# w2 transposed by DMA transposes on SyncE instead of on TensorE, and the products for M one step later

## Chip, cores and metric

The kernel runs on one core of a Trainium2 chip. The metric is the device time of one execution in microseconds (us). Before the change it is 490.49 us, the median of 3 runs (489.95 to 490.56).

## What is computed

```python
def _attn_ref(x, filt_r, filt_i):              # x: 8 x 3072 x 256
    X = np.fft.rfft(x, axis=1)
    F = (filt_r + 1j * filt_i)[None, :, :]
    return np.fft.irfft(X * F, n=x.shape[1], axis=1)

def _moe_ref(x, w1, w2, w_out):                # x: 24576 x 256, w1, w2: 256 x 1024, w_out: 1024 x 256
    h1 = x @ w1
    h2 = x @ w2
    g = np.maximum(h1, h2)
    return g @ w_out
```

The first function mixes along the sequence, with a filter in the frequency domain. Its result, reshaped to 24576 x 256, goes through the second.

## The kernel before

**The second part is rewritten.** Because max(h1, h2) = max(h1 - h2, 0) + h2, the kernel keeps the difference Wd = w1 - w2 and the product M = w2 @ w_out (256 x 256), and computes relu(y @ Wd) @ Wo + y @ M. So w2 itself is needed only for Wd and for M. To compute M on TensorE, w2 must lie with its 1024 columns on the partitions: that is w2T, w2 transposed.

**The work is a list of steps written out by hand.** After a setup (tables, and the mixing of batch 0), a loop runs over 64 tiles `tt` of 384 rows (8 per batch) and 8 steps `j` in each; step 8 * i + j of batch b is named (b, step). At each step the loop emits `moe_h(tt, j)` (two matmuls at L656, their ReLU on ScalarE at L661 or VectorE at L658), then what the dictionary `mid` holds for the step, then some matmuls of `moe_o(tt - 1, ...)` (L720 with Wo, L718 with M), then what `todo` holds for it, in the order in which `plan(b, step, fn, ...)` was called. Every engine takes its own instructions in this order, with no scheduler in between; semaphores only make it wait.

**Around the change**, in batch 0:

- GpSimd casts the second weight to bf16 in two halves, `cast_w2` (L327), into `w2b`. These casts come after its loads of x for batch 1 (L125), the load of w_out (L330) and the four pieces of Wd (L334).
- `prep_t(jp)` (L336) handles one of these halves: eight 128 x 128 transposes on TensorE into a PSUM tile (L341), and one eviction on ScalarE into `w2T` (L342). `prep_t(0)` is planned at step 7; `prep_t(1)` stands in `mid[0, 8]`, ahead of step 8's L720.
- `prep_m` (L344), at step 9, multiplies w2T by w_out: 16 matmuls (L348) and an eviction into M on ScalarE (L350). M is first read by L718 in step 12.
- `f1(1, c)` (L366, evicted at L369 or L371, stored on SyncE at L374 after every second c) is the first stage of batch 1, at steps 5 to 12. `f1_read` (L380) reads the stored rows back at step 13, and L435 uses them as `bt` from step 25 on. L366 of c = 8 to 11 reads the x tile of one GpSimd load, and of c = 12 to 15 that of the next.
- `load_xf` (L130, L134) on SyncE loads x of batch 2 from step 8 on; GpSimd's `fold` (L140, L141) takes these tiles, and L397 multiplies them from step 25 on.
- `t2` (L793) are other transposes on TensorE, for batch 0.

All SyncE DMAs go out in program order; a DMA whose input isn't ready holds up those behind it. At step 9, `prep_m` is planned ahead of `f1`, so its matmuls stand ahead of that step's L366.

Of the kernel before, what the change touches and what calls it, by code (L numbers as in the profile page):

```python
# [9 lines left out]
BF16 = mybir.dt.bfloat16  # L10
AF = mybir.ActivationFunctionType
# [4 lines left out]
D = 256  # L16
# [11 lines left out]
def kernel(  # L28
# [14 lines left out]
    nc = tc.nc  # L43
    V, S, G, TE = nc.vector, nc.scalar, nc.gpsimd, nc.tensor
# [11 lines left out]
    I128 = const.tile([128, 128], BF16)  # L56
# [3 lines left out]
    w2b = pfpool.tile([128, 2, HID], BF16, tag="pf", name="w2b")  # L60
    w2T = pfpool.tile([128, 8, D], BF16, tag="pf", name="w2T")
# [11 lines left out]
    ps = banks.enter_context(tc.tile_pool(name="ps", bufs=6, space=bass.MemoryType.PSUM))  # L73
# [35 lines left out]
    def plan(b, step, fn, *a):  # L109
        todo.setdefault((b + step // 64, step % 64), []).append((fn, a))  # L110
# [223 lines left out]
        engine.tensor_tensor(Wd[:, :, js], w1f[:, :, js], w2f[:, :, js], OP.subtract)  # L334

    def prep_t(jp):  # L336
        pt = ps.tile([128, 4, D], BF16, tag="ps", name="pt")
        for ji in range(4):
            for dc in range(2):
                j = 4 * jp + ji  # L340
                TE.transpose(pt[:, ji, 128 * dc:128 * dc + 128], w2b[:, dc, 128 * j:128 * j + 128], I128)  # L341
        S.activation(w2T[:, 4 * jp:4 * jp + 4], pt, AF.Copy)  # L342

    def prep_m():  # L344
        pm_ = ps.tile([128, 2, D], FP32, tag="ps", name="pm_")
# [566 lines left out]
    mid = {}  # L912
# [12 lines left out]
                plan(b, n, s1_read, b + 2, v)  # L925

    plan(0, 1, t2, 1, (V,))
    plan(0, 7, prep_t, 0)
    plan(0, 9, prep_m)
    for c, n in ((2, 7), (4, 22), (5, 32), (6, 40), (7, 48)):  # L930
        plan(0, n, t2, c, (V,))
    plan_f1(0, 1, (5, 6, 7, 7, 9, 9, 10, 10, 11, 11, 12, 12), 13)
# [37 lines left out]
    for b in range(B + 1):  # L970
        for i in range(8):
# [12 lines left out]
            assert sum(n) == 30  # L984
            share[b, i] = n

    mid[0, 8] = [(t2, (3, (V,))), (prep_t, (1,))]

    for tt in range(8 * B + 1):
        if tt == 7:  # L990
# [58 lines left out]
```

## Time and profile before

| | |
|---|---|
| median of 3 runs | 490.49 us |
| the profiled execution's own time | 489.1 us |
| its span, first to last instruction | 487.3 us |
| mean granted TensorE clock | 0.993 |
| w2b casts on GpSimd, L327 | 2 x 1.04 us, from 40.16 us |
| transposes of w2, L341 | 16, from 41.25 to 43.8 us |
| ScalarE evictions into w2T, L342 | 2 x 1.02 us |
| products for M, L348 | 16, from 45.0 to 46.6 us |

The profile shows one execution. PE is TensorE's matmuls, PEld its weight loads, DVE VectorE, ACT ScalarE, POOL GpSimd; SPq are the DMAs that SyncE issues. A row of the timeline gives start, length, engine, line, operation, and in brackets the idle time before it with what released it. The chain of work that ended last is followed back from the end of the run; its pieces add up without overlap, while matmul rows of the timeline overlap because matmuls are pipelined. A row of the stages gives the stretch, its length, busy time of the five engines with instruction counts, the granted TensorE clock (1.00 is full speed), the mean busy share of the 16 DMA engines, and GB/s.

### The profile page before, as it was taken

How to read it: one execution, taken by the hardware profiler on the slowest of the kernel's cores; microseconds unless marked ns; L12 is line 12 of the kernel's file. 1: busy time of each engine (PE TensorE's matmuls, PEld its weight loads, DVE VectorE, ACT ScalarE, POOL GpSimd, SP SyncE). 2: the span in 40 equal slices, each digit the busy share in tenths (PEclk: the TensorE clock that was granted, in tenths of full speed). 3: DMA queues.
4: the chain of work that ended last, by engine and by line, in shares of the span. 5: the costliest groups of instructions: out<-in, count | busy, mean ns of one | idle time of the engine just before them, and what ended most of it. 6: DMA issues, size and time to landing. Idle time of an engine off the chain costs nothing.

```text
span 487.3 us, 15411 instructions
## 1 busy us (share of the span) xinstructions
PE 475.9 (98%) x6204; PEld 342.3 (70%) x6207; DVE 362.4 (74%) x589; ACT 307.4 (63%) x645; POOL 296.0 (61%) x378
## 2 busy tenths in 40 slices
PE   8689999999999999999999999999999999999996
PEld 4457777776677676776677676776777776777775
DVE  7886789987876878677786778777885878775542
ACT  5877488667764778468764677467774556354442
POOL 8695868559980698739874698738951266111110
PEclk9979999999999999999999999999999999999999
DMA  8999999898766889789876897789556523541112
GB/s 124 172 247 228 263 255 270 272 254 241 216 180 193 214 270 282 222 237 265 234 187 199 237 261 222 221 245 248 169 165 213 175 88 107 174 156 66 66 66 86
DMA packets 87816, 97.37 MB, mean 200 GB/s; under 512 B 9281, under 2 KB 67938, under 8 KB 87650
## 3 DMA queue, kind: packets, MB, share of 16 engines
q1 hardware_dynamic: 79010, 79.30, 57.7%
q0 software_dynamic: 8592, 17.01, 13.8%
q8 instruction: 48, 0.79, 0.7%
q14 instruction: 22, 0.18, 0.1%
q10 hardware_dynamic: 144, 0.09, 0.1%
HBM read 53.87 MB, written 47.19 MB: 207 GB/s over the span
## 4 chain that ended last, share of the span: by engine, by line
PE 93%; DVE 2%; DMA 2%; POOL 1%; issue 1%; ACT 0%; DVEq 0%; POOLq 0%
PE po L720 36%; PE ph L656 34%; PE po L718 9%; PE pc L612 3%; PE pa L403 2%; PE pz L547 2%; PE px L493 2%; DMA xb<-in_x_dram 2%; DVE pq L441 1%; DVE F L164 1%; PE pr L793 1%; POOL xb L125 1%; PE pz L459 1%; PE pa L366 1%; PE py L629 1%
## 5 line engine op out<-in xcount | busy, mean ns | idle before, releaser
L720 PE MATMUL po<-Wo,gt 128*128 128x256 bf16 x1528 | 263.1, 273 | 0.0
L661 ACT ACTIVATE gt<-ph 128x384 bf16<-128x384 f32 x347 | 165.9, 502 | 141.6 <-PE ph L656 136.8
L720 PEld LDWEIGHTS <-gt 128*128 128x128 bf16 x1528 | 144.2, 98 | 66.4 <-issue 12.4
L658 DVE TENSOR_SCALAR gt<-ph 128x384 bf16<-128x384 f32 x165 | 90.6, 552 | 46.2 <-PE ph L656 44.5
L656 PEld LDWEIGHTS <-Wd 128*128 128x128 bf16 x1024 | 99.0, 98 | 14.1 <-DVE pf L507 0.7
L668 POOL DMA_DIRECT2D out_dram<-ot x86 | 48.8, 568 | 98.1 <-DVE ot L731 87.8
L140 POOL TENSOR_TENSOR xb<-XF 128x512 bf16<-128x512 f32 x48 | 61.1, 1274 | 51.3 <-DMA XF<-in_x_dram 44.4
L503 DVE TENSOR_TENSOR pf<-px,F 128x1024 f32<-128x1024 f32 x60 | 71.1, 1218 | 18.7 <-PE px L493 7.0
L731 DVE TENSOR_SCALAR ot<-po 128x512 f32<-128x512 f32 x83 | 57.0, 686 | 18.8 <-PE po L720 18.2
L141 POOL TENSOR_TENSOR xb<-XF 128x512 bf16<-128x512 f32 x48 | 61.0, 1272 | 0.0
L407 ACT ACTIVATE at<-pa 128x512 bf16<-128x512 f32 x96 | 50.0, 603 | 4.0 <-PE pa L403 3.1
L533 POOL TENSOR_TENSOR ri<-pf 128x256 bf16<-128x256 f32 x60 | 43.8, 730 | 14.3 <-DVE pf L503 14.1
L534 POOL TENSOR_TENSOR ri<-pf 128x256 bf16<-128x256 f32 x60 | 43.6, 727 | 0.0
L556 ACT ACTIVATE zt<-pz 128x512 bf16<-128x512 f32 x60 | 31.3, 600 | 9.2 <-PE pz L547 9.2
L617 ACT ACTIVATE ce<-pc 128x384 f32<-128x384 f32 x56 | 23.7, 490 | 3.5 <-PE pc L612 2.1
L441 DVE TENSOR_TENSOR pq<-px,F 128x1024 bf16<-128x1024 f32 x19 | 22.1, 1219 | 2.6 <-PE px L435 2.3
L403 PE MATMUL pa<-xb,CT 64*32 64x512 bf16 x320 | 16.2, 381 | 0.0
L612 PEld LDWEIGHTS <-zr 48*128 48x128 bf16 x896 | 12.6, 93 | 4.4 <-issue 3.6
L612 PE MATMUL pc<-G,zr 48*128 48x48 bf16 x896 | 14.8, 180 | 0.0
L493 PE MATMUL px<-bt,U 64*32 64x256 bf16 x432 | 14.4, 272 | 0.0
L514 DVE TENSOR_TENSOR pf<-px,F 128x1024 f32<-128x1024 f32 x6 | 7.4, 1226 | 5.0 <-POOL ri L534 4.3
L804 PE MATMUL pd<-W 128*128 128x512 bf16 x26 | 9.5, 496 | 1.5 <-DVE zero L186 1.5
(415 smaller groups left out, 735.5 us busy)
## 6 DMA issues: line engine op xcount, KB each, us to landing
XF<-in_x_dram SPq DMA_DIRECT2D x96, 192.0 KB
out_dram<-ot SPq DMA_DIRECT2D x101, 128.0 KB
out_dram<-ot POOLq DMA_DIRECT2D x90, 128.0 KB, 3.5
ad<-at SPq DMA_DIRECT2D x56, 192.0 KB
zd<-zt SPq DMA_DIRECT2D x42, 256.0 KB
bt<-ad SPq DMA_DIRECT2D x72, 128.0 KB
zr<-zd SPq DMA_DIRECT2D x24, 192.0 KB
zr<-zd SPq DMA_DIRECT2D x28, 96.0 KB
```

The lines of the kernel that those rows point to most:

```text
L140: G.tensor_tensor(t_[:, 0], f[:, 0], f[:, 1], OP.add)
L141: G.tensor_tensor(t_[:, 1], f[:, 0], f[:, 1], OP.subtract)
L407: S.activation(at[:, m0:m0 + 2], pa[g], AF.Copy)
L503: V.tensor_tensor(t_, px[s].rearrange("p (o k) d -> p o k d", o=1).to_broadcast([128, 2, 2, D]), F[:, :, 2 * n, s].rearrange("p c (o d) -> ...
L533: G.tensor_tensor(ri[:, s, 0], t_[:, 0, 0], t_[:, 1, 1], OP.subtract)
L656: TE.matmul(ph, Wd[:, dc, 128 * j:128 * j + 128], y_[:, dc], start=(dc == 0), stop=(dc == 1))
L658: V.tensor_scalar(gt[tt][:, j], ph, 0.0, None, OP.max)
L661: S.activation(gt[tt][:, j], ph, AF.Relu)
L668: E.dma_start(out=dst, in_=src)
L718: TE.matmul(p_, y_[:, n, blk], M[:, n], start=(e == 0), stop=(e == 9))
L720: TE.matmul(p_, g_[:, n - 2, blk], Wo[:, n - 2], start=(e == 0), stop=(e == 9))
L731: V.tensor_scalar(ot[tt // 2][:, e - 1:e + 1], po[q // 2 % 2], SCALE, None, OP.mult)
```

## The change

`prep_t` no longer uses TensorE, PSUM or ScalarE: for each half of w2 it issues two DMA transposes on SyncE, from w2b straight into w2T. The halves are planned at steps 3 and 4 instead of 7 and 8, so they stand on SyncE ahead of the stores of steps 6 and later. `prep_m` moves from step 9 to step 10.

```diff
     def prep_t(jp):
-        pt = ps.tile([128, 4, D], BF16, tag="ps", name="pt")
-        for ji in range(4):
-            for dc in range(2):
-                j = 4 * jp + ji
-                TE.transpose(pt[:, ji, 128 * dc:128 * dc + 128], w2b[:, dc, 128 * j:128 * j + 128], I128)
-        S.activation(w2T[:, 4 * jp:4 * jp + 4], pt, AF.Copy)
+        for dc in range(2):
+            nc.sync.dma_start(out=w2T[:, 4 * jp:4 * jp + 4, 128 * dc:128 * dc + 128],
+                              in_=w2b[:, dc, 512 * jp:512 * jp + 512], transpose=True)
...
     plan(0, 1, t2, 1, (V,))
-    plan(0, 7, prep_t, 0)
-    plan(0, 9, prep_m)
+    plan(0, 3, prep_t, 0)
+    plan(0, 4, prep_t, 1)
+    plan(0, 10, prep_m)
...
-    mid[0, 8] = [(t2, (3, (V,))), (prep_t, (1,))]
+    mid[0, 8] = [(t2, (3, (V,)))]
```

## The prediction

> **What bounds the kernel now.** I read the page's first part, then the chain of work that ended last, then that chain in order of time around the transposes. All three say TensorE:
>
> ```profile
> span 487.3 us, 15411 instructions
> PE 475.9 (98%) x6204; PEld 342.3 (70%) x6207; DVE 362.4 (74%) x589; ACT 307.4 (63%) x645; POOL 296.0 (61%) x378
> PE 93%; DVE 2%; DMA 2%; POOL 1%; issue 1%; ACT 0%; DVEq 0%; POOLq 0%
> ```
>
> TensorE is busy for 98% of the span and carries 93% of the chain. So I look at the stretch that the change touches, piece by piece (start, length, what):
>
> ```profile
> 41.32 0.55 PE pt L341 x8
> ...
> 43.53 0.45 PE pt L341 x8
> 43.98 0.44 PE po L720 x4
> 44.41 0.33 PE ph L656 x2
> 44.74 0.44 PE po L720 x4
> 45.17 1.75 PE pm__1160 L348 x16
> 46.92 0.43 PE pa L366 x2
> 47.35 0.33 PE ph L656 x2
> 47.68 0.44 PE po L720 x4
> 48.12 0.43 PE pa L366 x2
> ...
> 50.07 0.33 PE po L718 x3
> ```
>
> Every piece from 41 to 50 us is TensorE's, end to end. What leaves TensorE here shortens the run by its length, and a wait put into its queue lengthens the run by its length, because TensorE takes its instructions in order and everything behind the wait stands still.
>
> **Removed.** Two groups of eight transposes: 0.55 + 0.45 = **1.00 us** of the chain. ScalarE loses two evictions too:
>
> ```profile
> L342 ACT ACTIVATE w2T<-pt x2: 1024/1024/1024, 41.9 to 44.0; 128x1024 bf16<-128x1024 bf16 x2
> ACT gt L661 <- PE ph L656: 6.1, 9, 1.7
> ```
>
> That is 2.05 us of ScalarE's time, but between 30 and 70 us ScalarE itself waited 6.1 us in 9 waits for TensorE (second row), so I count nothing for it. The two PSUM tiles that go free are counted at nothing as well: no TensorE wait in this stretch names one.
>
> **Moved.** The products for M (L348, 1.75 us) pass behind one step's L366, L656 and L720. Moved alone, they would start at 48.12 - 1.75 = **46.37**; without the transposes, at 46.37 - 1.00 = **45.37**. If S is the time at which they really start, the run changes by **S - 46.37**, as long as nothing later is late. M is next needed by L718: in the new order 50.07 - 48.12 = 1.95 us of other matmuls stand between the products' end and it, and ScalarE's copy of M takes 0.60 us:
>
> ```profile
> 46.96 0.60 ACT L350 ACTIVATE M<-pm__1160 128x512 bf16<-128x512 f32 x1 [1.92 <-PE pm__1160 L348]
> ```
>
> So the copy stays hidden with 1.3 us to spare.
>
> **Exposed by the move.** L366 of step 9, which stood behind the products, now comes first, at 46.92 - 1.75 - 1.00 = 44.17. It reads the x tile of one GpSimd load:
>
> ```profile
> 35.42 1.06 POOL L125 DMA_DIRECT2D xb<-in_x_dram  x2
> DMA to landing us min/median/max: 9.4/9.4/9.4
> DMA to landing us min/median/max: 9.4/10.2/11.0
> ```
>
> The second row is the answer for the first of these two loads alone, the third for both: the first lands at 35.42 + 9.4 = 44.82. So TensorE waits 0.65 us there, and S can't be below 44.82 + 0.43 + 0.33 + 0.44 = **46.02**. Two thirds of what the transposes free is given back to this load before w2T is even looked at. The second, for steps 11 and 12, is issued 0.53 us later and lands at 47.0; step 11's L366 stands behind the products, so not before 46.02 + 1.75 = 47.8.
>
> **Added.** Four DMA transposes of 128 KB each on SyncE. Two of them need the first half of w2b, two the second:
>
> ```profile
> 40.16 2.02 POOL L327 CAST w2b<-WS 128x1024 bf16<-128x1024 f32 x2
> 37.35 0.68 DVE L369 CAST at<-pa 96x512 bf16<-96x512 f32 x1
> 36.80 7.21 SPq L374 DMA_DIRECT2D ad<-at  x4
> 44.06 0.56 SPq L130 DMA_DIRECT2D XF<-in_x_dram  x1
> ```
>
> The casts end at about 41.20 and 42.18. VectorE's part of the second store is done at 38.03, so SyncE has sent that store by about 38.4 and stands, in the new order, at the wait for the first cast. What one transpose costs the trace doesn't show. The nearest rows are the four copies from SBUF to SBUF, also 128 KB and also from SyncE, and for the landing the two places where somebody waited for SyncE's transfers while the DMA engines were full:
>
> ```profile
> 20.45 3.83 SPq L166 DMA_DIRECT2D F<-F  x4
> L166 SPq EVENT_SEMAPHORE  x4: 17/17/648, 20.4 to 23.1; - x4
> L166 SPq DMA_DIRECT2D F<-F x4: 507/594/1216, 20.5 to 23.8; - x4
> 46.35 0.43 SPq L134 DMA_DIRECT2D XF<-in_x_dram  x1
> 50.17 1.27 POOL L140 TENSOR_TENSOR xb<-XF 128x512 bf16<-128x512 f32 x1 [7.20 <-DMA XF<-in_x_dram]
> 51.80 0.82 SPq L374 DMA_DIRECT2D ad<-at  x2
> L380 SPq EVENT_SEMAPHORE  x1: 28/28/28, 55.7 to 55.7; - x1
> 42.00:44.00 2.00, 2.00 (x28) 1.67 (x27) 1.64 (x3) 1.80 (x3) 0.85 (x4) 1.00 1.06 244
> 44.00:46.00 2.00, 2.00 (x20) 1.69 (x19) 0.81 (x2) 1.02 (x1) 0.00 (x0) 1.00 0.97 286
> ```
>
> The four copies took 3.83 us less 0.70 us of semaphore waits, 0.78 us each. From the end of the last issue to the landing it was 50.17 - 46.78 = 3.4 us for the load and 55.7 - 52.6 = 3.1 us for the stores. The DMA share (last but one number of the stage rows) is 1.06 and 0.97 in the very microseconds of the transposes, so I take the loaded landing, 3.4.
>
> - Value taken: 41.20 + 4 x 0.78 (the second half's cast is done before its turn comes at 42.77) = 44.33 issued, + 3.4 = 47.73 landed. S = 47.73, change **+1.36 us**.
> - Lower end: 4 x 0.51 and 3.1: 46.33 landed, change -0.04. If the transposes land earlier still, the x load holds S at 46.02: -0.35. If that load comes earlier too (it shares the DMA engines with SyncE's XF loads, which now start later), -1.00 is the floor.
> - Upper end: 4 x 1.22 and 3.4: 49.5 landed, change +3.1. With the 11.0 us that the second x load took to land, 55.3 and +9.0.
>
> I take the middle value because the copies have the transposes' size, queue and endpoints; both ends stay in the range.
>
> [...]
>
> **Behind the waiting SyncE.** The stores of steps 6 and 7 and all XF loads stand behind the transposes. The loads start at 44.33 + 2 x 0.33 = 44.99, not 44.06. Who waits for them is GpSimd's fold and the read of bt:
>
> ```profile
> 51.40 1.27 POOL L141 TENSOR_TENSOR xb<-XF 128x512 bf16<-128x512 f32 x1
> 56.12 2.18 SPq L380 DMA_DIRECT2D bt<-ad  x3
> 61.38 0.41 PE L435 MATMUL px<-bt,U 64*64 64x256 bf16 x8
> 61.62 0.39 PE L397 MATMUL pa<-xb,CT 64*64 64x512 bf16 x4
> ```
>
> The first folded tile is complete at 52.67, or 0.9 us later, and L397 wants it at 61.62. The read of bt moves to 57.1 at most, and L435, which wants it at 61.38, moves by 1.4 us itself. Neither ends last. The transposes' 0.5 MB at the 244 GB/s of that stage row are 2.1 us of DMA time, by which the x load can be late: 46.9 instead of 44.82, then 1.20 us of matmuls, 48.1. That lies 0.4 us behind the taken S and is inside the case's range.
>
> **Sum.** -1.00 (transposes) + 0.65 (x load) + 1.71 (w2T after that) = +1.36 us. Against the profiled execution's own 489.1 us (its 487.3 us of span and 1.8 around it) that is 490.5. The median of the runs is 490.49, 1.4 us above the profiled one, so I forecast **491.9 us**, 0.28% slower. About 0.2%, 1.0 us, is what a measurement can tell from no change.
>
> **The rivals.**
>
> - *The wait stays small* (S from 45.4 to 47.35, change within 1.0 us): 489.5 to 491.5 us, typically 490.5. For it: the lower end above, and the floor that the x load sets at -0.35. Against it: four issues and a loaded landing must fit into the 6.15 us from the first cast to 47.35, and the rows give 6.5.
> - *A crossbar transpose is no copy* (landing after about 50): SyncE or the DMA engines take several times a copy's time. With the 11.0 us landing the change is +9.0. Then TensorE stands for over 8 us, and the clock joins in:
>
> ```profile
> 22.00:23.00 1.00, 0.00 (x0) 0.00 (x0) 1.00 (x1) 0.97 (x2) 0.00 (x0) 1.00 0.81 225
> 24.50:25.00 0.50, 0.35 (x27) 0.22 (x34) 0.50 (x2) 0.50 (x2) 0.50 (x1) 0.50 0.32 82
> 31.50:32.00 0.50, 0.24 (x18) 0.27 (x19) 0.50 (x2) 0.45 (x1) 0.50 (x1) 1.00 1.08 348
> ```
>
>   After a thin stretch around 22 to 24 us the granted clock (the third number from the end) stood at 0.50 from before 24.5 until shortly before 31.5: 7 us at half speed cost up to 3.5 us. Together +12.5, 503 us. For it: no row shows a transpose, and it rewrites every 2-byte element's place, which a copy doesn't. Against it: only the neighbourhood of copies. [...]
> - *Faster*: the x load lands by 44.17 because the XF loads come 0.9 us later, and w2T by 45.37. Then TensorE never waits and all of the 1.00 us is kept: 489.5 us. It decides at 45.37: four issues and the landing in 4.17 us. Against it: four issues at the smallest 0.51 leave 2.1 us for the landing, and no loaded landing here is under 3.1.
>
> **How the numbers follow.** Forecast case (S 47.35 to 50, 491.5 to 494.1 us) 0.38; small wait 0.31; no copy 0.25; faster 0.06. Slower by over 0.2% is 0.38 + 0.25 = 0.63, within 0.31, faster 0.06. The range starts at 490.0, which leaves out the faster case and a little of the small wait, and reaches to 498.0, which takes in the forecast case and the nearer half of the slow one, with an eighth above it.
>
> **What would show it.** In the changed kernel's chain: L341 gone; L366 around 44.2 with an idle time whose releaser is the xb load, of 0.6 us or more; L348 idle until the w2T DMA, starting near 47.7; L718 with no wait for M. On SyncE: four new rows of about 0.8 us from 41.2. If those rows are 2 us and more, the third case holds; if L348 doesn't wait, one of the other two. Wrong altogether would be an L348 that starts early and a run that is still slower: then something behind SyncE's queue ends last.

## The result and the profile after

The changed kernel takes **496.39 us** (median of 6 runs, 494.59 to 498.48) against 490.36 (6 runs, 489.49 to 491.66): 1.24% slower, ratio 1.0124, 95% interval 1.0096 to 1.0152. The profiled execution took 495.99 us. The new line numbers are three below the old ones: L363 is the old L366, L345 the old L348, L717 the old L720, L715 the old L718, L432 the old L435, L371 the old L374. L338 issues the transposes.

The page after, the lines that answer to those shown of before:

```profile
span 494.2 us, 15385 instructions
PE 476.0 (96%) x6188; PEld 341.0 (69%) x6191; DVE 362.5 (73%) x589; ACT 305.2 (62%) x643; POOL 296.5 (60%) x378
DMA packets 89992, 97.90 MB, mean 198 GB/s; under 512 B 11457, under 2 KB 70114, under 8 KB 89826
PE 84%; DMA 7%; POOL 4%; SPq 2%; DVE 1%; issue 1%; POOLq 0%; DVEq 0%
```

TensorE's share of the chain fell from 93% to 84%; DMA, GpSimd and SyncE took over. TensorE's timeline shows where (start, length, what, and in brackets the idle time and what ended it):

```profile
36.69 0.62 PE L790 MATMUL pr<-I,zT 128*96 128x128 bf16 x8 [0.34 <-DVE zT L777]
44.21 0.61 PE L790 MATMUL pr<-I,zT 128*96 128x128 bf16 x8
45.66 0.60 PE L717 MATMUL po<-Wo,gt 128*128 128x256 bf16 x4 [0.84 <-DMA Wo<-in_moe_w_out_dram]
47.53 0.63 PE L363 MATMUL pa<-xb,C 96*96 96x512 bf16 x2 [0.51 <-DMA xb<-in_x_dram]
50.71 0.61 PE L345 MATMUL pm__1161<-Wo,w2T 128*128 128x256 bf16 x4 [1.78 <-DMA w2T<-w2b]
51.73 1.48 PE L345 MATMUL pm__1161<-Wo,w2T 128*128 128x256 bf16 x12 [0.42 <-DMA w2T<-w2b]
53.05 0.60 PE L363 MATMUL pa<-xb,C 96*96 96x512 bf16 x2
68.22 0.41 PE L432 MATMUL px<-bt,U 64*64 64x256 bf16 x8 [1.68 <-DMA bt<-ad]
```

TensorE now waits in four places for a DMA: w_out, the x load, w2T, and bt. The same places before:

```profile
35.11 0.62 PE L793 MATMUL pr<-I,zT 128*96 128x128 bf16 x8 [0.34 <-DVE zT L780]
42.92 0.61 PE L793 MATMUL pr<-I,zT 128*96 128x128 bf16 x8
43.81 0.60 PE L720 MATMUL po<-Wo,gt 128*128 128x256 bf16 x4
46.76 0.60 PE L366 MATMUL pa<-xb,C 96*96 96x512 bf16 x2
47.95 0.60 PE L366 MATMUL pa<-xb,C 96*96 96x512 bf16 x2
```

From start to start this gives a balance, with the first L790 (L793) as zero, so that the 1.58 us by which this execution's setup was longer stay out of it:

| stretch | before | after | difference |
|---|---|---|---|
| first to fourth group of t2 (holds transposes of the first half) | 7.81 | 7.52 | -0.29 |
| to the first L717 (held those of the second half) | 0.89 | 1.45 | +0.56 (w_out) |
| to step 9's L363, products (1.75) left out | 1.20 | 1.87 | +0.67 (x load) |
| to step 10's L363, with the products | 2.94 | 5.52 | +2.58 (w2T) |
| to the first L432 | 13.43 | 15.17 | +1.74 (bt) |
| sum | 26.27 | 31.53 | **+5.26** |

The rest of the span's 6.9 us is the setup's 1.58 and 0.1 after that. SyncE's rows:

```profile
42.52 7.55 SPq L338 DMA_TRANSPOSE w2T<-w2b  x4
L338 SPq DMA_TRANSPOSE w2T<-w2b x4: 1305/1452/3139, 42.5 to 46.9; - x4
51.21 0.44 SPq L130 DMA_DIRECT2D XF<-in_x_dram  x1
63.77 2.40 SPq L377 DMA_DIRECT2D bt<-ad  x3
```

Four transposes hold SyncE for 7.55 us. The XF loads start at 51.21, not 44.06, and the read of bt goes out at 63.77, not 56.12; 1.58 us of each is the later setup. Followed back from L432, the chain of work that ended last has these among its pieces (start, length, what):

```profile
46.93 3.14 SPq L338
54.15 5.40 DMA XF<-in_x_dram
60.06 3.66 DMA ad<-at
63.77 4.41 DMA bt<-ad
```

It runs from the last transpose over the XF loads, the last store and the read of bt, and the products for M aren't in it. The balance says where TensorE lost its time; this chain says what set the start of L432 in this execution.

The stages show what the DMA engines did meanwhile (last two numbers: their busy share and GB/s):

```profile
46.00:48.00 2.00, 1.49 (x11) 0.84 (x9) 0.56 (x1) 0.01 (x1) 0.00 (x0) 1.00 1.36 202
48.00:50.00 2.00, 0.93 (x7) 0.49 (x5) 0.69 (x1) 1.02 (x2) 0.00 (x0) 1.00 1.54 39
```

The last of these stages before:

```profile
48.00:50.00 2.00, 2.00 (x15) 1.27 (x13) 1.03 (x3) 1.95 (x5) 0.00 (x0) 1.00 0.96 226
```

From 48 to 50 us the engines count as more than fully busy, with 1.54, and move 39 GB/s. The page of before has 9281 packets under 512 bytes, this one 11457: 2176 more, 544 for each transpose, whose 128 KB thus go in pieces of about 240 bytes on average.

### The profile page after: what moved, and what is told of

Its sections match the earlier page's. It is cut to its first block, busy times and chain, and to the rows that moved or that the text cites. A ratio compares the mean times of both kernels' runs of the same rounds, so it can differ in the third digit from the quotient of the medians.

```text
span 494.2 us, 15385 instructions
## 1 busy us (share of the span) xinstructions
PE 476.0 (96%) x6188; PEld 341.0 (69%) x6191; DVE 362.5 (73%) x589; ACT 305.2 (62%) x643; POOL 296.5 (60%) x378
## 2 busy tenths in 40 slices
DMA packets 89992, 97.90 MB, mean 198 GB/s; under 512 B 11457, under 2 KB 70114, under 8 KB 89826
## 4 chain that ended last, share of the span: by engine, by line
PE 84%; DMA 7%; POOL 4%; SPq 2%; DVE 1%; issue 1%; POOLq 0%; DVEq 0%
PE po L717 33%; PE ph L653 31%; PE po L715 8%; PE pc L609 3%; PE pa L400 2%; PE pz L544 2%; PE px L490 2%; DMA xb<-in_x_dram 2%; POOL pq L438 1%; SPq L338 1%; POOL xb L125 1%; DMA XF<-in_x_dram 1%; DMA bt<-ad 1%; DVE F L164 1%; POOL Wd L334 1%
## 5 line engine op out<-in xcount | busy, mean ns | idle before, releaser
L717 PE MATMUL po<-Wo,gt 128*128 128x256 bf16 x1528 | 263.0, 273 | 0.8 <-DMA Wo<-in_moe_w_out_dram 0.8
L717 PEld LDWEIGHTS <-gt 128*128 128x128 bf16 x1528 | 144.3, 98 | 67.4 <-issue 13.4
L490 PE MATMUL px<-bt,UN 64*32 64x256 bf16 x144 | 10.3, 269 | 0.0
```

What stands on the lines that cost most here:

```text
L717: TE.matmul(p_, g_[:, n - 2, blk], Wo[:, n - 2], start=(e == 0), stop=(e == 9))
```

## The experiments

The theory: the loss is the transposes' hold on SyncE and on the DMA engines, and it reaches TensorE through whatever stands behind them and is wanted soon. The rivals: the move of the products, the setup, or single waits that add up one by one. Times are medians with the ratio to the kernel before and its 95% interval.

**The move alone.**

```diff
-    plan(0, 9, prep_m)
+    plan(0, 10, prep_m)
```

> The kernel before with only the products for M moved from step 9 to step 10, TensorE still transposing. Theory: the move costs nothing by itself, since the x load at 44.8 us lands just before L366 wants it at 45.2: 490.4 us, within 0.3 of before. Rival (the move itself exposes TensorE to the x load): slower by 0.65 us or more.

Measured: 490.42 us, ratio 1.0003 (0.9988 to 1.0018). The move costs nothing by itself.

**Everything but the transposes.** The products read w2b, untransposed, so M is another matrix.

```diff
-    plan(0, 3, prep_t, 0)
-    plan(0, 4, prep_t, 1)
...
-                TE.matmul(pm_[:, dc], w2T[:, j, 128 * dc:128 * dc + 128], Wo[:, j],
+                TE.matmul(pm_[:, dc], w2b[:, dc, 128 * j:128 * j + 128], Wo[:, j],
```

> The changed kernel without its four DMA transposes; the products for M read w2b where they read w2T, so M is computed from w2 not transposed. Theory (the transposes' own time on SyncE makes both waits, for w2T and for bt): both vanish, and against the kernel before 1.00 us of TensorE's transposes less 0.65 to 1.3 us of waiting for the loads of x and w_out remains: 490.0 to 490.7 us, no L432 wait for bt. Rival (the later start of everything in the changed profile, 1.3 to 1.8 us at 36 us, belongs to the change): 491.5 us or more, with the casts of w2 starting at 41.5 us again instead of 40.2.

Measured: 490.94 us, ratio 1.0014 (1.0001 to 1.0027), just above the theory's range. Three rows of TensorE in this profile (a row without brackets has no wait of note), the group of GpSimd's casts, and a wait much later:

```profile
36.26 0.62 PE L790 MATMUL pr<-I,zT 128*96 128x128 bf16 x8 [0.34 <-DVE zT L777]
45.76 0.63 PE L363 MATMUL pa<-xb,C 96*96 96x512 bf16 x2
62.17 0.41 PE L432 MATMUL px<-bt,U 64*64 64x256 bf16 x8
L327 POOL CAST w2b<-WS x2: 1031/1031/1031, 41.6 to 42.6; 128x1024 bf16<-128x1024 f32 x2
210.34 0.75 PE L609 MATMUL pc<-G,zr 48*128 48x48 bf16 x47 [0.50 <-DMA zr<-zd]
```

From the first L790 to L432 it is 25.91 us, before 26.27: of the 1.00 us of transposes only 0.36 is kept, close to the 0.35 that the prediction left after the x load. The casts start at 41.6, as late as in the changed kernel, yet the span is 488.8. So the waits for w2T and bt go with the transposes. From L432 to the end this profile takes 426.63 us, before 425.92; 0.50 of that is the wait for a read of zr in the last row. Why the median shows no gain at all stays open.

**The transposes issued, nobody waiting for w2T.** Only the second edit of the run above.

> The changed kernel with all four DMA transposes issued as they are, but the products for M read w2b, so nothing waits for w2T (and M is computed from w2 not transposed). Theory (SyncE's queue sets the end: stores and the read of bt stand behind the transposes): L345 no longer waits, but L432 waits for bt all the longer, some 4.5 us instead of 2.1, starts again near 68.2 us, and the time stays within 0.5 us of the changed kernel's 496.4. Rival (the two waits add): the 2.2 to 2.5 us of the wait for w2T are saved, about 494.0 us.

Measured: 496.31 us, ratio 1.0118 (1.0086 to 1.0150), the time of the changed kernel. L345 doesn't wait any more; L432 does, and its wait is longer:

```profile
65.36 0.64 PE L432 MATMUL px<-bt,U 64*64 64x256 bf16 x8 [3.70 <-DMA bt<-ad]
66.00:68.00 2.00, 2.00 (x12) 1.04 (x8) 1.96 (x2) 1.08 (x2) 1.69 (x2) 0.50 1.08 303
```

The theory's time holds, its mechanism only in part. L432 starts at 65.4, not at 68.2 as expected: the setup was 1.21 us shorter, and L432 had bt 2.86 us after its read went out, not 4.45. From the first L790 to L432 it is 29.88 us, against 31.53 in the changed kernel, so 1.65 us of the wait for w2T was given back in this execution. But with the wait of 3.7 us the granted clock fell to 0.50 (third number from the end) and stayed low until about 71.5, which took it again: from L432 to the end this profile takes 429.74 us, the changed kernel's 425.98. Through the waits of 1.78 and 1.68 us in the changed kernel's profile it had stayed at 1.00. Here it fell at about 64.7 us, some 3.0 us after the wait began, and in the next run it fell behind a wait of 2.69 us.

**Three XF loads behind the read of bt.**

```diff
-              (8, 8, 10, 12, 17, 20, 24, 28), (10, 13, 16, 20, 24, 27, 30, 33))
+              (8, 14, 15, 16, 18, 20, 24, 28), (10, 16, 18, 20, 24, 27, 30, 33))
```

> The changed kernel with three of the four XF loads of steps 8 to 12 planned behind the read of bt, so that on SyncE only one stands between the transposes and the last stores. Theory (two waits one behind the other): the wait for w2T stays at 2.2 us, the read of bt goes out about 3 us earlier and L432's wait of 2.1 us vanishes: 494.3 us. Rival (bt is late because the DMA engines are full, not because of SyncE's order): L432 still waits 1.5 us or more, 496 us.

Measured: 501.68 us, ratio 1.0230 (1.0208 to 1.0253). Both expectations missed. TensorE's timeline and then GpSimd's:

```profile
50.62 3.37 PE L345 MATMUL pm__1157<-Wo,w2T 128*128 128x256 bf16 x16 [2.69 <-DMA w2T<-w2b]
73.21 0.37 PE L394 MATMUL pa<-xb,CT 64*64 64x512 bf16 x1 [2.25 <-POOL xb L140]
71.90 1.26 POOL L140 TENSOR_TENSOR xb<-XF 128x512 bf16<-128x512 f32 x1 [10.34 <-DMA XF<-in_x_dram]
```

L432 no longer waits for bt, as the theory had it: its wait did come from SyncE's order. But now the next consumer of the queue waits, L394 for the folded x. The products took 3.37 us instead of 1.75, at half clock (0.50 from 51 to 53 us), and behind L394 the clock fell once more (0.52 from 74 to 76 us).

**Copies instead of transposes** (w2T then holds w2 not transposed).

```diff
-                              in_=w2b[:, dc, 512 * jp:512 * jp + 512], transpose=True)
+                              in_=w2b[:, dc, 512 * jp:512 * jp + 512].rearrange("p (j d) -> p j d", j=4))
```

> The changed kernel with the four transposes replaced by four plain copies of the same 128 KB from w2b to w2T, in the same places of SyncE's queue, so that w2T holds w2 not transposed. Theory (a crossbar transpose is no copy: 6.5 to 7.5 us of SyncE for four, where copies take some 3): SyncE is free by about 45 us, L345 waits 1 us or less, L432 doesn't wait, 490.4 to 491.5 us. Rival (any 512 KB put there makes the loads of x and the stores late, because the DMA engines are full): 494 us or more, with L432 waiting for bt.

Measured: 493.82 us, ratio 1.0086 (1.0061 to 1.0111). Between the two expectations, and nearer the rival:

```profile
L338 SPq DMA_DIRECT2D w2T<-w2b x4: 672/712/1594, 41.8 to 44.1; - x4
46.31 0.63 PE L363 MATMUL pa<-xb,C 96*96 96x512 bf16 x2 [0.88 <-DMA xb<-in_x_dram]
48.70 0.61 PE L345 MATMUL pm__1161<-Wo,w2T 128*128 128x256 bf16 x4 [1.00 <-DMA w2T<-w2b]
46.00:48.00 2.00, 1.40 (x8) 0.75 (x8) 0.69 (x1) 1.03 (x2) 0.00 (x0) 1.00 1.08 231
```

The copies hold SyncE half as long (3.89 us) and move 231 GB/s where the transposes had 202 and 39, with nearly the same number of packets (11393 under 512 bytes on the page). The loads of x and w2T are late all the same. From the first L790 to L432 this profile takes 28.80 us: 2.53 more than before, where the changed kernel's has 5.26 more. So a part of the loss comes with half a megabyte of copies at this place, in pieces of about 250 bytes on average (2112 packets under 512 bytes more than before), and more because it is transposed. The sizes are loose: by the medians the copies cost 3.9 of the 6.0 us, but their interval and that of the changed kernel (1.0096 to 1.0152) overlap, the runs spread from 492.49 to 496.42, and the profiled one, the slowest, lost another 4.0 us behind L432, most of it at 177 to 185 us, where TensorE waited three times and the clock fell to 0.50.

**Half of them.** The second half goes through TensorE again, at step 8; only step 3's two DMA transposes stay.

```diff
-    plan(0, 4, prep_t, 1)
...
-    mid[0, 8] = [(t2, (3, (V,)))]
+    mid[0, 8] = [(t2, (3, (V,))), (prep_te, (1,))]
```

> The changed kernel with only the first half of w2 transposed by DMA (two transposes, step 3) and the second half by TensorE as before (step 8). Theory (the loss is SyncE's time under the transposes beyond what the kernel can hide, so it is no straight line): SyncE is held about 3 us instead of 7, w2T is whole by 47 to 48 us, L345 waits 0 to 1 us, bt is on time, 490.4 to 491.6 us. Rival (the loss goes with the number of transposes): half of the 6 us, about 493.4 us.

Measured: 495.15 us, ratio 1.0092 (1.0066 to 1.0119). The theory's number is wrong; the rival's, 493.4, lies at the lower end of the interval. SyncE was held 2.69 us, as expected, but:

```profile
42.78 2.69 SPq L338 DMA_TRANSPOSE w2T<-w2b  x2
50.03 1.92 PE L353 MATMUL pm__1169<-Wo,w2T 128*128 128x256 bf16 x16 [2.65 <-DMA w2T<-w2b]
66.92 0.41 PE L440 MATMUL px<-bt,U 64*64 64x256 bf16 x8 [1.64 <-DMA bt<-ad]
```

The last of the two was issued by 45.47 and landed at about 50.0, 4.5 us later. So SyncE's time isn't the whole price: a transpose can land long after SyncE is free of it.

**Two transposes of 256 KB instead of four.**

```diff
-        for dc in range(2):
-            nc.sync.dma_start(out=w2T[:, 4 * jp:4 * jp + 4, 128 * dc:128 * dc + 128],
-                              in_=w2b[:, dc, 512 * jp:512 * jp + 512], transpose=True)
+        dc = jp
+        nc.sync.dma_start(out=w2T[:, :, 128 * dc:128 * dc + 128], in_=w2b[:, dc], transpose=True)
```

> The changed kernel with two DMA transposes of 256 KB instead of four of 128 KB, both after the second cast. Theory (SyncE's time goes with the bytes, 1.25 us for 128 KB and more under load): each row takes 2.5 us or more, the wait for w2T and the one for bt stay, 495.5 to 497.5 us. Rival (SyncE's time is one price for each DMA): rows of about 1.3 us, SyncE free 2 to 4 us earlier, 493.5 us or less.

Measured: 493.73 us, ratio 1.0072 (1.0053 to 1.0090). The rows, then the wait:

```profile
L338 SPq DMA_TRANSPOSE w2T<-w2b x2: 1534/2799/4064, 42.3 to 43.9; - x2
49.21 3.03 PE L344 MATMUL pm__1159<-Wo,w2T 128*128 128x256 bf16 x16 [2.38 <-DMA w2T<-w2b]
```

The time is close to the rival's, the rows to neither: 5.66 us of SyncE for the same bytes, in a row of 1.53 and one of 4.06. That is as much as four transposes took in the shortest other case (5.73 us, with the XF loads moved), so the number of DMAs isn't the price; what sets it instead, this run doesn't show. L432 doesn't wait.

**One transpose in quiet.** The kernel before, with four more transposes in the last batch.

```diff
+    def extra_t(jp):
+        o_ = F.rearrange("p c w s d -> p (c w s d)")[:, 0:2048].rearrange("p (j d) -> p j d", j=8)
+        for dc in range(2):
+            nc.sync.dma_start(out=o_[:, 4 * jp:4 * jp + 4, 128 * dc:128 * dc + 128],
+                              in_=Wd[:, dc, 512 * jp:512 * jp + 512], transpose=True)
+
+    for jp in range(2):
+        plan(7, 20 + jp, extra_t, jp)
```

> The kernel before with four more DMA transposes of 128 KB, from Wd into the filter's tile, which nobody reads any more, planned at steps 20 and 21 of the last batch, where the DMA engines are busy for a tenth to two tenths. It measures the price of one transpose by itself. Theory (SyncE is held by the transpose's own work, not by full DMA engines): each row takes 1.2 us or more here too. Rival (full DMA engines held SyncE): 0.5 to 0.7 us each, like a copy. The time stays within 0.3 us of before unless the output stores behind them are late.

Measured: 490.17 us, ratio 1.0005 (0.9993 to 1.0016).

```profile
L966 SPq DMA_TRANSPOSE F<-Wd x4: 1242/1267/1353, 446.0 to 451.1; - x4
447.00:449.00 2.00, 2.00 (x18) 1.51 (x16) 1.07 (x2) 0.78 (x2) 0.00 (x0) 1.00 0.70 178
```

As the theory had it, each row takes 1.24 to 1.35 us where the DMA engines have room (their share from 445 to 453 us is 0.20 to 0.70, and 0.13 to 0.34 in the kernel before), twice a copy's 0.51 to 0.59 at the lower end and the middle. Under load single rows reach 3 to 6 us: 3.14 in the changed kernel, at a share of 1.36 and 1.54, and 6.31 in the next run, at 1.14 to 1.53.

**Ahead of everything.** A version that was to keep the gain: w2b loaded by a DMA that casts, the transposes where SyncE idles, the products ahead of L363 again.

```diff
             load_x(1, 0, 2)
+            G.dma_start(out=w2b, in_=moe_w2.rearrange("(c p) j -> p c j", p=128))
+            for jp in range(2):
+                prep_t(jp)
...
-    for h in range(2):
-        cast_w2(h)
...
-    plan(0, 3, prep_t, 0)
-    plan(0, 4, prep_t, 1)
-    plan(0, 10, prep_m)
+    plan(0, 9, prep_m)
```

> A version meant to keep the gain: w2b is loaded from memory by one GpSimd DMA that casts, beside the first load of x for batch 1, so that GpSimd's two casts of 1.03 us go too; the four transposes stand ahead of the first store on SyncE, where it idles from 28 to 37 us; the products for M are back at step 9, ahead of L366. Theory (the place in SyncE's queue is what costs): no wait for w2T or bt, TensorE's 1.00 us is kept, 489.2 to 489.8 us. Rival (transposes or the added 1 MB read take DMA time from the loads of the weights and x wherever they stand): Wd or x come late, 491 us or more.

Measured: 502.00 us, ratio 1.0250 (1.0234 to 1.0266). The rival holds, and by far:

```profile
36.45 11.39 SPq L338 DMA_TRANSPOSE w2T<-w2b  x4
L338 SPq DMA_TRANSPOSE w2T<-w2b x4: 1321/1808/6312, 36.5 to 41.5; - x4
Wo<-in_moe_w_out_dram POOLq DMA_DIRECT2D x1, 512.0 KB, 16.5
43.23 0.50 PE L653 MATMUL ph<-y__1006,Wd 128*128 128x384 bf16 x2 [1.86 <-POOL Wd L334]
50.96 0.60 PE L717 MATMUL po<-Wo,gt 128*128 128x256 bf16 x4 [3.81 <-DMA Wo<-in_moe_w_out_dram]
```

The stage from 34 to 50 us is where w_out and the last loads of x for batch 1 arrive. The load of w_out took 16.5 us to land, 9.2 before, and one transpose held SyncE for 6.3 us, from 41.5 on, with the engines' share at 1.14 to 1.53. SyncE's idle time there is no free place: in the kernel before, the DMA engines' share is already 1.07 to 1.24 from 36 to 42 us. How much is due to the transposes and how much to the added load of w2, this run doesn't separate.

**Behind the read of bt.** Transposes at step 14, products reading w2b.

```diff
-    plan(0, 3, prep_t, 0)
-    plan(0, 4, prep_t, 1)
...
+    for jp in range(2):
+        plan(0, 14, prep_t, jp)
...
-                TE.matmul(pm_[:, dc], w2T[:, j, 128 * dc:128 * dc + 128], Wo[:, j],
+                TE.matmul(pm_[:, dc], w2b[:, dc, 128 * j:128 * j + 128], Wo[:, j],
```

> The same four DMA transposes, but planned at step 14, behind the read of bt in SyncE's queue, and the products for M read w2b, so that nothing waits for w2T (M is computed from w2 not transposed). Theory (what costs is what stands behind the transposes and is wanted soon: w2T and the read of bt): no wait for either, and the time is that of the kernel without transposes, 490.2 to 491.6 us. Rival (the transposes' hold on the DMA engines costs wherever they stand in a busy stage): 493 us or more, with L432 or L394 waiting for what lands late.

Measured: 491.88 us, ratio 1.0043 (1.0021 to 1.0066), just above the theory's range: 0.9 us above the kernel without transposes, a difference that these runs can't tell from none for certain, and far below the 496.31 of the run with w2T unread, which differs from this one only in the transposes' place.

```profile
60.16 7.33 SPq L338 DMA_TRANSPOSE w2T<-w2b  x4
99.55 0.76 PE L609 MATMUL pc<-G,zr 48*128 48x48 bf16 x47 [0.90 <-DMA zr<-zd]
212.50 0.19 PE L609 MATMUL pc<-G,zr 48*128 48x48 bf16 x1 [1.16 <-DMA zr<-zd]
```

The same transposes hold SyncE as long, and neither w2T nor bt is waited for. What is left are waits for reads of zr, much later on the same queue; that the transposes cause these was not tried, and shorter ones (0.41 and 0.50 us) stand in the profiles of the move alone and of the run without transposes too. So the place decides most of the price.

**Both kernels once more.**

> The changed kernel once more, for a second profile. If the later setup of its first profile (casts of w2 from 41.5 us, not 40.2) belongs to the change, the casts start at 41.4 to 41.6 again; if it varies from one execution to the next, anywhere from 40.2 to 41.7. Four transposes hold SyncE 5.7 to 7.6 us again, L345 and L432 wait 1.5 us or more each.

> The kernel before once more, for a second profile. If the setup varies by execution, the casts start anywhere from 40.2 to 41.7 us and the span is 487.3 plus that difference; if the early setup belongs to this program, 40.2 again.

Measured: 495.17 us and 489.68 us, one run each. The casts start at 40.6 us in both. So the late setup of the first profile after belongs to the execution, not to the change. In the second profile after the waits lie elsewhere than expected, and SyncE is held longer:

```profile
41.69 8.55 SPq L338 DMA_TRANSPOSE w2T<-w2b  x4
48.76 1.09 PE L363 MATMUL pa<-xb,C 96*96 96x512 bf16 x2 [2.30 <-DMA xb<-in_x_dram]
67.03 0.41 PE L432 MATMUL px<-bt,U 64*64 64x256 bf16 x8 [0.19 <-DMA bt<-ad]
```

The x load is the late one, 2.30 us, the products behind it find w2T landed, and bt is late by 0.19. Matmuls at a clock of 0.50, from 49 to 52 us, follow here too. From the first L790 to L432 it is 31.34 us, against 26.16 in the second profile before: the loss, 5.18, is that of the first pair. Which transfer ends last differs between the two profiles; that they are late together doesn't.

## Why the prediction was right, and where not

**The time was inside the range, but not in the forecast case.** The forecast was 1.4 us slower, and 6.0 were measured. 496.39 lies in the third case, that a transpose is no copy, which had a chance of 0.25 ("crossbar" is the prediction's word, and no run here shows what a transpose goes through); the range held because it took in that case's nearer half. Up to step 10's L363 the profile lost 3.52 us where the sum had 1.36, and on to L432 another 1.74, which the prediction had put at nothing.

**The direction and the first wait were right.** The products for M wait for w2T, and their waits of 1.78 and 0.42 us made their stretch longer by 2.58. M itself is not waited for by L715, as worked out. The move alone costs nothing.

**Removed, 1.00 us; the x load takes 0.65 of it back: right in sum, partly by luck.** Without transposes 0.36 us is kept up to L432, against 0.35. But the x load took only 0.28 of it (1.48 us from L717 to step 9's L363, against 1.20); most of the rest went ahead of it, in the stretch of the first half, which is 7.57 us against 7.81.

**Added, 4 x 0.78 us on SyncE: too low.** Measured 7.55 us in the first profile, and 5.7 to 8.6 in the others with four at this place. The nearest row, a copy, was the wrong yardstick: a transpose took 1.24 us and more even in quiet, and up to 4.00 us in the profiles with four at this place, where the engines' share was 0.80 to 1.68. The landing after the last issue was shorter than the 3.4 us taken (50.07 to 51.73 is 1.66); with half of the transposes it was 4.5. In sum the second half landed 9.2 us after the first cast ended (42.49 to 51.73), not 6.5: that is the term that was mis-sized, 2.7 us. The third case was the rival with the right reason, and its landing after about 50 us came true; its size, +9.0 us and the clock, was too much.

**Behind the waiting SyncE, "Neither ends last": wrong.** With SyncE held until 50.07, not 44.33, the read of bt comes 7.7 us later (1.58 of them the setup's), where the prediction had 1.0 at most, and L432 waits 1.68. The run with w2T unread shows that this chain, with the clock that its longer wait loses, is enough for a loss of the same size.

**The x load late by up to 2.1 us: right in kind, the bound too small.** From its issue to its landing it took 10.8 us in the first profile and 12.8 in the second, against 9.4 before: 1.4 and 3.4 later. With it came a wait for w_out that the prediction didn't have (0.84 us). The 2.1 us were worked out from the bytes at 244 GB/s; with the transposes the stage moved 39. The pieces' size alone doesn't explain that, as the copies in like pieces moved 231.

**The clock** joins in already at waits of 2.3 to 3.8 us, where the prediction kept it for 8 us. The first profile after doesn't show it; the second one does, with 0.50 after 2.30 us, and so do five of the experiments, the copies only at 180 us, behind three waits of 0.43 to 0.83; with half of the transposes the clock stayed at 1.00 beside a wait of 2.65 us, so that the length of the wait alone doesn't decide it. Of the six runs of the changed kernel the two slowest, 498.48 and 498.29 us, have the lowest mean granted clock, 0.986 and 0.983; that fits, but neither was profiled.

What stays open: why the kernel without transposes has no gain in its median, 490.94 us, although its profile is ahead at L432; and how much of the loss is SyncE's hold and how much the engines', which no run here separates: the half-size run shows that a transpose can be late without much hold, and the run with XF loads moved that the queue's order matters.

No version here beats the kernel before.

## What to carry to other kernels

Here four transposes were taken off the bounding engine and given to the DMA engines, and their place on the queue set most of their price. With w2T unread it was 496.31 us ahead of the read of bt and 491.88 behind it, though the DMA engines' share reached 1.66 in the one stage and 1.54 in the other; in quiet four more cost nothing (490.17). So follow the queue behind the new transfer to each consumer, with the new operation's own price and not that of the nearest copy, and look at the busy share of the DMA engines in the microseconds where it will stand. Several transfers were late together here, and taking away the wait for bt only showed the next one, 2.25 us at L394.

## What the runs showed of the hardware

- A DMA transpose of 128 KB between two places in SBUF held SyncE for 1.24 to 1.35 us where the DMA engines' share was 0.20 to 0.70, and for 1.23 to 6.31 us where it was 0.80 to 1.68 (medians of the profiles 1.27 to 1.81 us).
- It went as 544 packets, all under 512 bytes (the 2176 that the page after has more than that of before, over four), and a stage with these packets showed a busy share of 1.54 at 39 GB/s; copies in pieces of nearly the same size had 1.08 at 231 GB/s.
- The granted clock fell to 0.50 with a single wait of 3.70 us, and came back about 7 us later; it fell to 0.50 with waits of 2.30, 2.38 and 2.69 us too in three other profiles, and stayed at 1.00 beside one of 2.65 us.
